# The memory update of a segmented attention block: one full-array product for a group of heads, or one column tile for each head's quadrant

## The chip, the cores and the metric

The kernel runs on one core of a Trainium2 chip. The core has TensorE (PE, with its weight loads as a row of their own, PEld), VectorE (DVE), ScalarE (ACT), GpSimd (POOL) and SyncE (SP, which only issues DMAs). The metric is the device time of one execution in microseconds, as a median over runs. Profiles come from one execution each.

## The reference

A pre-norm transformer block on 2048 tokens of 640 values: attention with 32 heads of 20 values, in four segments of 512 tokens, and a feed-forward part of 1728. Inside a segment the attention is a causal softmax; what earlier segments had is read through a memory M (20 x 20 a head) and its normaliser z, which are updated after each segment.

```python
phi = lambda t: jnp.where(t > 0, t + 1.0, jnp.exp(t))
for s in range(N):
    logits = jnp.einsum('bhqd,bhkd->bhqk', qs, ks) * scale + mask
    a_dot = jnp.einsum('bhqk,bhkd->bhqd', _softmax(logits, axis=-1), vs)
    pq = phi(qs)
    num = jnp.einsum('bhld,bhde->bhle', pq, M)
    den = jnp.einsum('bhld,bhd->bhl', pq, z)[..., None] + 1e-06
    outs.append(g * num / den + (1.0 - g) * a_dot)
    pk = phi(ks)
    M = M + jnp.einsum('bhld,bhle->bhde', pk, vs)
    z = z + jnp.einsum('bhld->bhd', pk)
h = x + concat(outs) @ wo
h2 = h + silu(layernorm(h) @ w1) @ w2
```

## The kernel before

**Layout.** The projections q and k put the 640 values into five tiles of 128 rows. A tile has four quadrants of 32 rows; quadrant r of tile c holds the 20 values of head 4c+r and 12 rows out of the heads 20 to 31, which are cut into pieces. `Vx` holds the values of a segment with a column of ones behind each head (VS = 21 columns a head, V4 = 84 for four heads), so that one product gives M and z.

**The work of a segment.** Layer norm and transposes (n1_), projections of v (v), q and k (pr), their evacuation (qe), phi of q and k (ex on ACT, then pa and pb on DVE, L844 and L850), eight ticks of four heads, the output projection (wo, rs), a second layer norm (n2_), and the feed-forward part (h1, th, s, h2, o, out). A tick has scores (qk, L900), their exponentials (e, ACT, L913), the causal masks (mk, POOL, L925), the product with the values (av, L948), its scaling (oe, L963), the transposition together with the reading of the memory (tn, L977 and L981) and the normalisation (nm, ad).

**The memory update**, `declare_memory`, once after each of the segments 0, 1 and 2, for each of the five tiles c: a DMA transpose of phi(K) into `phiKt` (kt, L1049, on SP's queue), four products (mz, L1057; eight for c = 4), one addition into the running sum `Mz` (ma, DVE; L1083 copies in segment 0, L1086 adds later), and one product with a constant mask `MzM` on POOL that writes the bf16 operand `Mzb` of the next segment's ticks (mb, L1093). A product takes a whole tile, 128 columns of phi(K) transposed, as weights and moves the values of two or three groups of four heads (168 or 252 columns) through it. So each quadrant meets the values of all four heads of a group, and the mask then keeps only the blocks where a quadrant met its own head. Each tile has a PSUM bank of its own for this and an `Mz` buffer of its own.

**The order.** There is no scheduler at run time. Each piece of work is a task with a name, such as `mz03` (segment 0, tile 3) or `ma03`; the string `ORDER` lists all of them, with the buffer slots and, after a slash, the engine (`/A` ACT, `/D` DVE, `/G` POOL, `/S` SP). Each engine gets its instructions in the order of the list and waits in order; semaphores come from a tracker of reads and writes. `/C` marks a TensorE task that is written as column tiles: each full-array matmul (128*128, L545) becomes four on 32 columns each (128*32, L546) that lie side by side in the array. The scores use row tiles (20*128), av and the last h1 of a segment column tiles, the rest the full array.

Of the kernel before, what the change touches and what calls it, by code (L numbers as in the profile page):

```python
# [327 lines left out]
D = 640  # L328
# [34 lines left out]
zpad:0 iota epsc vpad1 mt0 x0:0 mta0 mtb0 halfc sel mt3 n1_st0:6 x1:1 n1_rs0 n1_st1:1 x2:2 x3:3 w_q:0 n1_st2:3 n1_rs1  # L363
n1_rs2 n1_st3:5 fill20:0 n1_rs3 re_wq0/G:0 re_wq1/G n1_ap1:0 n1_ap2:2 mm2 w_k mt1 warm:0 re_wk1/G:0 fill9:0 n1_tp1:4
mm9 re_wk2/G n1_ap0:3 n1_ap3:0 w_wv:0 n1_tp2:2 n1_tp0:0 mm6 n1_tp3:6 n1_te3/D:2 vpad0 mta3 beta n1_te1/A n1_te2/A mta1
re_wq2/G n1_te0/A re_wk0/A x4/A:4,5,6,7 mtb3 re_wk3/G pr000.0:6 pr000.1 qe000/A:0 pr010.0:1 pr001.0:2 re_wk4/A pr001.1
qe001/D pr011.0:7 pr011.1 zf0 zf1 mm8 qe011/D:0 pa011:1 re_wq3/G qk0a0:4,2 lsc0 lsc1 x8/A:8,9,10,11 ex001:1 re_wq4/G
pa001:2 pb001 kt00:0 mzc9 e0a0:4 pr010.1 qe010/D e0a2 mtb1 pr021.0:7 pr021.1 qe021/D:0 n1_st4:4 n1_rs4 v00.0:6 pa021:0
ex011:2 qk0b0:3,1 e0b0:5 e0b2 mk0b w_w1_3/S:0 w_w1_4/S pb011 v01.0:0 mm1 n1_st5:5 v00.1 ve00/A:0 pr020.0:5 pr020.1
qe020/A v01.1 n1_rs5 vt09:0 ex021:1 vt03 w_w2_5/S qk0e0:2,6 e0e2:0 v02.0:4 v02.1 v03.0:6 e0e0 n1_st6:6 ve01/D ve02/A  # L370
n1_st9:1 qk1a0:2,0 n1_ap5:2 n1_rs6 v03.1 n1_ap6:0 e1a0:1 pr031.0:4 pr031.1 kt01:1 n1_tr5:0 vt00 e1a2 n1_tr6 ve03/D
qk1b0:2,5 e1b0:6 e1b2 pb021 qe031/D:0 w_w1_0/S pr030.0:7 pr030.1 n1_ap4:3 n1_tr4 pr041.0:4 mk1a qk2a0:2,0 n1_st10:3
lsc2 mzc6 pa031:1 qe030/D pr041.1 qe041/D:0 ex031:1 pr040.0:5 pr040.1 vt06 e2a2:3 qe040/D vt08 vt04 e2a0 qk2b0:6,0
e2b0:2 vt07 lsc3 mk0e mk1b mz00:4 mk0a ma00/D:0 pb031 vt02 n1_rs10 av1:3 e2b2 oe1/D:1 mm5 mm11 mzc5 av0:2 oe0/D:0 mm0
qk2e0:4,6 e2e0:6 mz01:0 ma01/D:2 tn0:2 qk3a0:4,0 e2e2 mt2 e3a2:0 nm0:1,0 tn1:3 nm1:1 v10.0:2 v10.1 mk2b n1_st7:5
ve10/D:1 kt02:0 e3a0 mk2a n1_st11:6 qk3b0:0,6 mk2e vt05 e3b2:1 n1_rs7 e3b0 vt01 av2:5 oe2/D:1 mm3 mk3a qk4a0:6,2
mz02:4 ma02/D:3 mk3b v11.0:0 e4a2:2 vt010 e4a0 qk4b0:2,4 n1_rs9 mta2 mm4 n1_ap7:3 n1_st8:5 n1_rs8 kt03:1 e4b0:4 e4b2
vt011 v11.1 ve11/D mk4b tn2:7 nm2:1 pa041:2 mz03:6 ex041:2 qk4e0:2,0 e4e0:3 av3:7 e4e2 mk4a n1_tr7 epsg0 pr100.0/C:4
pr100.1/C ma03/D:4 oe3/D:0 qk5a0:2,6 mzc1 e5a0:5 mk4e pr110.0:5 pb041 e5a2 kt04:0 qe100/D:0 pr110.1 pr120.0:4
qe110/D:0 qk5b0:2,0 pa110:0 mtb2 av4:5 oe4/D:1 pa100:0 pr120.1/C mzc2 n1_ap10:3 n1_tr10:2 e5b2:6 qk6a0:0,6 w_w1_1/S  # L380
mz04:5 qe120/D:0 e5b0 ma04/D:1 v12.0:2 tn3:4 nm3:2 n1_ap8:1 e6a2:4 v12.1 ve12/D e6a0 tn4:7 ex100:1 pb100 nm4:2
qk6b0:4,0 pr101.0:6 e6b2:0 mk5b pr101.1 e6b0 qk6e0:0,2 e6e2:1 mk5a av5:7 n1_rs11 pa120:0 mzc0 e6e0 pr111.0/C:4 qe101/D
w_w2_3/S pr111.1/C qk7a0:2,5 e7a0:3 e7a2 n1_ap9:3 oe5/D:0 pr130.0:7 n1_tr8 qe111/D tn5:0 pa111:2 mm7 v13.0:4 nm5:2
pr130.1 qe130/D:0 qk7b0:2,0 mzc7 mzc3 mb01:0 mk6b v13.1/C ex111:1 pb111 mk6e mk6a av6:6 n1_tr9 mzc4 ve13/D e7b2:5
pr140.0/C:7 pr140.1/C qk8a0:0,4 pa101:1 oe6/D:0 pr121.0:6 pr121.1 e7b0 qe140/D:0 tn6:7 ex101:2 ex120:0 pb101 mb02:0
pb120 e8a0:4 mk7b e8a2 qk8b0:2,0 w_wo/S:0 e8b2:0 e8b0 mk7a qe121/D av7:6 nm6:0 pr131.0/C:7 oe7/D:1 kt10:1 qk8e0:0,4
e8e2:6 tn7:6 pa130:0 kt11:0 nm7:0 pr131.1/C qe131/D e8e0 mz11:2 ma11 qk9a0:5,3 mzc8 pr141.0:7 w_w2_4/S n1_ap11:3
vt10:0 mb03:0 e9a2:3 e9a0 ot0:1 mk8b mz10:1 ot1 mb00:0 ma10 pr141.1 pa121:0 mk8e qk9b0:0,2 e9b2:1 wo0.0:4 wo0.1 mk8a
av8:2 e9b0 mk9b ex131:2 qe141/D qk10a0:0,6 mk9a rs0 oe8/D:0 wo1.0:3 wo1.1 e10a0:2 e10a2 n2_st0:5 rs1 n2_st1:2 ot2
wo2.0:2 n2_rs0 ex110:0 qk10b0:0,5 e10b2:5 vt110 wo2.1 rs2 ot3 wo3.0:4 e10b0 wo3.1 pa131:2 ex121:1 qk10e0:2,0 e10e2:0  # L390
v20.0:6 v20.1 n2_rs1 n2_ap1:2 v21.0:0 e10e0 w_w1_2/S pb131 pb121 rs3 ve20/A:0 vt13 qk11a0:4,2 vt17 vt19 e11a0:4
n2_st2:1 vt15 v21.1 v22.0:6 tn8:4 e11a2 n1_tr11 n2_tr1:1 pb110 mk10a ex141:0 mk10b v22.1 w_w2_0/S n2_st3:7 n2_ap0:0
epsg1 nm8:3,1 vt16 v23.0:2 vt12 n2_rs2 ve22/A v23.1 n2_ap2:1 mk10e ve21/A ex140:2 n2_rs3 qk11b0:6,4 av9:0 ve23/D
ex130:1 e11b2:6 n2_ap3:3 oe9/D:1 av10:1 mzc11 vt14 oe10/D:0 pb130 e11b0 pr201.0/C:2 pr201.1/C qk12a0:0,4 e12a2:2
qe201/D:0 ex201:1 mk11a e12a0 mm10 tn9:6 n2_tr0 pr211.0:3 pr211.1 n2_tr2 n2_tr3 tn10:4 mzc10 mb04:0 ad8:0 nm9:3,0
qe211/A:0 nm10:0,1 vt11 pa141:1 h1_0_0_0.0:2 h1_0_0_0.1 mk11b av11:6 pa140:0 th0_0_0:0 s0_0_0:0 oe11/D:0 pb141
qk12b0:0,3 h1_0_1_0.0:7 h1_0_1_0.1 ad9 kt12:1 mz12:5 kt13:0 mz13:6 vt18 e12b2:1 tn11:2 e12b0 th0_1_0:1 vt111 ma12 ma13
qk12e0:4,0 e12e0:4 pr221.0:6 e12e2 ad10 s0_1_0 pr221.1 h1_0_2_0.0:7 h1_0_2_0.1 nm11:0,1 th0_2_0:0 qk13a0:3,1 e13a2:0
h1_0_3_0.0:5 mk12a mk12b h1_0_3_0.1 qe221/D:0 e13a0 pa211:2 pa201:0 pb201 mk12e kt14:0 mz14:6 pr231.0:2 s0_2_0 av12:7
ma14 th0_3_0:1 mk13a ex211:0 oe12/D:0 qk13b0:3,0 e13b0:2 e13b2 mk13b pr231.1 h1_0_4_0.0:6 s0_3_0 h1_0_4_0.1 th0_4_0:0  # L400
qe231/D:0 qk14a0:2,4 e14a2:1 w_w2_1/S h1_0_5_0.0:7 pb140 tn12:0 h1_0_5_0.1 e14a0 s0_4_0 pr200.0:6 pr200.1 th0_5_0:0
nm12:3,0 qk14b0:0,3 qe200/D s0_5_0 e14b0:3 av13:2 oe13/D:0 h1_0_6_0.0/C:5 h1_0_6_0.1/C qk14e0:1,6 e14b2 pr241.0:0
pr241.1 qe241/D:0 ad12 th0_6_0:1 h1_0_7_0.0:4 h1_0_7_0.1 e14e2:5 tn13:6 e14e0 s0_6_0 qk15a0:0,2 mk14b th0_7_0:0
e15a0:2 h1_0_8_0.0:5 e15a2 h1_0_8_0.1 s0_7_0 th0_8_0:0 nm13:2,0 mk14a h1_0_9_0.0:4 pb211 h1_0_9_0.1 pr210.0:7
qk15b0:0,2 mk14e av14:6 s0_8_0 pr210.1 oe14/D:1 ex200:1 e15b0:4 th0_9_0:1 s0_9_0 h1_0_10_0.0:1 kt20:0 h1_0_10_0.1
e15b2 ad13 mk15a qe210/D h1_0_11_0.0:0 qk16a0:4,2 th0_10_0:0 s0_10_0 tn14:6 nm14:1,0 h1_0_11_0.1 e16a2:0 e16a0
th0_11_0:0 h1_0_12_0.0:1 h1_0_12_0.1 th0_12_0:1 pa200:0 pb200 mk15b ad11 s0_11_0 qk16b0:6,3 e16b2:3 av15:5 oe15/D:1
pr220.0/C:2 pr220.1/C s0_12_0 e16b0 qe220/D h1_0_13_0:3 th0_13_0:0 pa221:0 s0_13_0 kt21:1 pa231:2 qk16e0:6,0 e16e0:5
tn15:4 pr230.0:2 ad14 nm15:2,0 pa210:0 pr240.0:3 e16e2 pr230.1 qk17a0:6,0 qe230/D mz20:4 mk16a mb10:0 ex221:0 ma20
e17a0:1 pr240.1/C mk16b qe240/D e17a2 mb11:0 mk16e qk17b0:4,6 e17b2:6 av16:2 ad15 mz21:3 pa240:0 oe16/D:0 mk17a  # L410
# [54 lines left out]
def build(nc, es, A_x, A_wq, A_wk, A_wv, A_wo, A_beta, B_x, B_w1, B_w2, out):  # L465
# [70 lines left out]
    def dve_c(n):  # L536
        return n / 960.0 + 0.067
# [172 lines left out]
    def layer_norm(tag, b, xa, xsub, dstA, i, prio):  # L710
# [31 lines left out]
        if tag == "n1_" and b < 4:  # L742
# [528 lines left out]
```

## Time and profile before

| | before |
|---|---|
| median of 3 runs | 301.94 us (301.9 to 303.04) |
| the profiled execution | 301.67 us |
| its span | 299.9 us |
| granted TensorE clock over the span | 1.00 |
| memory products, L1057 | 72 of 128x84 to 128x252, mean 200 to 270 ns each |
| additions, L1083 and L1086 | 15, of 168 or 252 elements, 5.4 us busy |
| masks, L1093 | 15, of 168 or 252 elements (542 and 719 ns), 9.2 us busy |
| transposes of phi(K), L1049 | 15, landing 3.2 us after their issue (median; 2.3 to 6.8) |

The length of a matmul row holds the time until its last result has landed, so matmuls overlap in the rows; what one costs the stream is the distance between the starts. Times in a timeline are counted from the start of the span. A row that begins with a line number gives the line, the engine, the operation, what it writes and reads, its tile shape (rows*columns of the array) and its data shape.

### The profile page before, as it was taken

Reading aid. Unit: us, or ns where it says so; the run is one execution under the profiler, and the core shown is the slowest. Engines: PE = TensorE matmul, PEld = TensorE weight load, DVE = VectorE, ACT = ScalarE, POOL = GpSimd, SP = SyncE. Lnnn points to the kernel's source line nnn. Section 1 sums busy time; section 2 is a strip of 40 time slices with the busy share of each in tenths; the row PEclk is TensorE's granted clock in tenths of the full one; section 3 lists DMA queues with packets and bytes.
Section 4 is the critical chain, followed back from the end, with each engine's and each line's share of the span. In section 5 each row is a group of like instructions: output and inputs, shape, how many; then the busy total and the mean of one; then the engine's idle time right before and its main releaser. Section 6 shows DMA issues by size and latency. Waiting matters only on the chain.

```text
span 299.9 us, 7708 instructions
## 1 busy us (share of the span) xinstructions
PE 284.8 (95%) x3134; PEld 158.7 (53%) x3160; DVE 222.5 (74%) x460; ACT 212.6 (71%) x273; POOL 150.0 (50%) x299
## 2 busy tenths in 40 slices
PE   8799889989989999999999999999999999999996
PEld 5354444435545444566654454555654557764574
DVE  6498988987999868879968975698545777726622
ACT  3699999999988999975788768877888741004400
POOL 5896886674665355746563752445863621300000
PEclk9999999999999999999999999999999999999999
DMA  7787524936663103064447220601511013321021
GB/s 212 260 258 115 118 48 103 216 75 150 166 101 89 20 2 87 5 96 80 80 93 125 46 44 7 112 2 23 61 40 30 2 48 65 71 63 44 1 90 44
DMA packets 48579, 24.68 MB, mean 82 GB/s; under 512 B 38880, under 2 KB 47456, under 8 KB 48544
## 3 DMA queue, kind: packets, MB, share of 16 engines
q1 hardware_dynamic: 47488, 22.88, 35.2%
q10 hardware_dynamic: 1056, 1.31, 1.4%
q8 instruction: 25, 0.41, 0.6%
q14 instruction: 10, 0.08, 0.1%
HBM read 10.41 MB, written 2.62 MB: 43 GB/s over the span
## 4 chain that ended last, share of the span: by engine, by line
PE 70%; DVE 14%; DMA 6%; ACT 6%; issue 2%; SPq 1%; POOL 0%; DVEq 0%; ACTq 0%
PE ps_all L545 48%; PE ps_all L546 6%; PE ps_all L900 6%; PE ps_all L948 4%; ACT PT L913 4%; DMA sT<-in_A_wk_dram 3%; DVE stt L720 2%; DMA x_tok<-in_A_x_dram 2%; PE ps_all L977 2%; DVE x_tok L1125 1%; PE ps_all L1057 1%; PE ps_all L981 1%; DVE sT L1166 1%; DVE phiQ L850 1%; DVE xn_rot L737 1%
## 5 line engine op out<-in xcount | busy, mean ns | idle before, releaser
L913 ACT ACTIVATE PT<-ps_all 128x1024 bf16<-128x1024 f32 x160 | 154.9, 1028 | 27.6 <-PE ps_all L900 24.7
L925 POOL TENSOR_SCALAR_AFFINE_SELECT PT<-PT 128x512 bf16<-128x512 bf16 x128 | 82.1, 648 | 63.2 <-ACT PT L913 59.9
L1160 ACT ACTIVATE th<-ps_all 128x512 f32<-128x512 f32 (+1 forms) x56 | 32.1, 591 | 35.9 <-PE ps_all L545 28.8
L545 PE MATMUL ps_all<-tT,w_sb 128*128 128x512 bf16 x224 | 53.8, 380 | 1.5 <-issue 0.5
L545 PE MATMUL ps_all<-w_sb,sT 128*128 128x320 bf16 x376 | 53.9, 299 | 0.0
L1166 DVE SCALAR_TENSOR_TENSOR sT<-th,ps_all 128x512 bf16<-128x512 f32 (+1 forms) x56 | 36.2, 662 | 16.9 <-ACT th L1160 16.3
L545 PEld LDWEIGHTS ps_all<-w_sb,sT 128*128 128x128 bf16 x376 | 35.9, 98 | 15.6 <-issue 1.5
L545 PEld LDWEIGHTS ps_all<-tT,w_sb 128*128 128x128 bf16 x233 | 21.0, 98 | 26.1 <-issue 2.8
L720 DVE BATCH_NORM_STATS2 stt<-x_tok 128x6 f32<-128x320 bf16 x64 | 28.0, 479 | 2.2 <-DMA x_tok<-in_A_x_dram 1.8
L1202 DVE SCALAR_TENSOR_TENSOR x_tok<-ps_all,x_tok 128x640 bf16<-128x640 f32 (+1 forms) x17 | 13.2, 781 | 19.9 <-PE ps_all L545 14.7
L1022 POOL TENSOR_TENSOR otok<-on 128x320 bf16<-128x320 bf16 x24 | 19.2, 801 | 12.7 <-DVE on L1014 12.7
L545 PE MATMUL ps_all<-wv_sb,tT 128*128 128x320 bf16 x155 | 24.3, 300 | 0.2
L963 DVE TENSOR_SCALAR oTs<-ps_all,lsc 128x512 bf16<-128x512 f32 x29 | 21.4, 744 | 3.8 <-PE ps_all L948 3.5
L545 PE MATMUL ps_all<-wo_sb,tT 128*128 128x320 bf16 x160 | 23.6, 299 | 0.6 <-DMA tT<-otok 0.6
L948 PE MATMUL ps_all<-PT,Vx 128*32 128x384 bf16 (+3 forms) x512 | 22.7, 301 | 1.2 <-DVE QK L831 0.7
L831 DVE CAST QK<-ps_all 128x512 bf16<-128x512 f32 x26 | 17.8, 686 | 7.0 <-PE ps_all L545 6.9
L1014 DVE TENSOR_TENSOR on<-ps_all,rd 128x640 bf16<-128x640 f32 x24 | 19.8, 825 | 1.3 <-POOL otok L1022 0.5
L729 POOL TENSOR_TENSOR rst<-mvt,eps_c 128x1 f32<-128x1 f32 x32 | 6.6, 207 | 27.8 <-DVE mvt L723 27.7
L545 PE MATMUL ps_all<-tT,wqr 128*128 128x512 bf16 x70 | 18.1, 379 | 2.2 <-DVE tT L756 1.2
L545 PE MATMUL ps_all<-tT,wkr 128*128 128x512 bf16 x72 | 18.8, 379 | 1.3 <-issue 1.1
L731 POOL TENSOR_TENSOR rst<-rst,eps_c 128x1 f32<-128x1 f32 x32 | 18.0, 563 | 2.5
L545 PEld LDWEIGHTS ps_all<-wo_sb,tT 128*128 128x128 bf16 x160 | 15.0, 98 | 7.8 <-issue 1.1
(86 smaller groups left out, 356.4 us busy)
## 6 DMA issues: line engine op xcount, KB each, us to landing
out_dram<-x_tok SPq DMA_DIRECT2D x15, 160.0 KB, 1.9
w_sb<-in_B_w_dram SPq DMA_DIRECT2D x5, 432.0 KB, 4.0
w_sb<-in_B_w_dram SPq DMA_DIRECT2D x3, 480.0 KB, 3.9
x_tok<-in_A_x_dram ACTq DMA_DIRECT2D x2, 640.0 KB, 4.9
QKV<-QK SPq DMA_DIRECT2D x12, 72.0 KB
sT<-in_A_wq_dram SPq DMA_DIRECT2D x1, 800.0 KB, 6.2
sT<-in_A_wk_dram SPq DMA_DIRECT2D x1, 800.0 KB, 8.0
wv_sb<-in_A_wv_dram SPq DMA_DIRECT2D x1, 800.0 KB, 9.6
```

The costliest lines, as they stand in the source:

```text
L545: return [lambda e: e.matmul(out, lhsT=lhsT, rhs=rhs, start=start, stop=stop)]
L546: return [lambda e, p=p: e.matmul(out[p:p + 32, :], lhsT=lhsT[:, p:p + 32], rhs=rhs, start=start, stop=stop, tile_position=(0, p)) for p i ...
L720: T.add(DV, lambda e, hh=hh: e.bn_stats(out=stt[:, s, 6 * hh:6 * hh + 6], in_=xb[:, 320 * hh:320 * hh + 320]), reads=R((xa, xsub)), writes ...
L731: T.add(PO, lambda e: e.tensor_tensor(out=rst[:, s, :], in0=rst[:, s, :], in1=eps_c[:, 1:2], op=ALU.pow), reads=R((st, ["r"]), (C, ["half" ...
L913: T.add(AC, lambda e: e.activation(out=pt[:, pta.slot, q0:q0 + 2, 0:width], in_=sc3[:, b0:b0 + 2, 0:width], func=ACT.Exp, scale=SCALE), re ...
L925: fns.append(lambda e, v=v: e.affine_select(out=v, in_=v, pattern=[[0, 4], [1, 128]], compare_op=ALU.is_ge, fill=0.0, base=0, channel_mult ...
L948: fns.append(lambda e, j=j, r=r, h=h, pa=pa, pt=pt, co=co, q0=q0, ji=ji: e.matmul(bank(po)[32 * r:32 * r + 32, q0:hi], lhsT=Vx[:, vx.slot, ...
L963: f = lambda e: e.tensor_scalar(out=o, in0=i_, scalar1=lsc[:, g:g + 1], scalar2=None, op0=ALU.mult)
L1014: T.add(DV, lambda e: e.tensor_tensor(out=on[:, ona.slot, :, :].rearrange("p b (x e) -> p b x e", e=DH), in0=v[:, :, :, 0:DH], in1=r2.unsq ...
L1022: T.add(PO, lambda e: e.tensor_tensor(out=o_dst, in0=on[:, ona.slot, 0, :].rearrange("p (i x) -> p i x", i=4), in1=on[:, ona.slot, 1, :].r ...
L1160: T.add(AC, lambda e: e.activation(out=th[:, tha.slot, lo:hi], in_=bank(ps)[:, lo:hi], func=ACT.Tanh, scale=0.5), reads=R((ps, [0])), writ ...
L1166: T.add(DV, lambda e: e.scalar_tensor_tensor(out=sT[:, f, lo:hi], in0=th[:, tha.slot, lo:hi], scalar=1.0, in1=bank(ps)[:, lo:hi], op0=ALU. ...
```

## The change

In `declare_memory` the four products of a tile become products in column tiles. A quadrant r of the transposed phi(K), 32 columns of `phiKt`, is the weight of one column tile, and only the values of its own heads move through it: two, three or one heads, 42, 63 or 21 columns. The four quadrants are written one after the other in the program as a group of four. Their results go to the rows 32r to 32r+31 of one PSUM bank, side by side with those of the other tiles: 12 pieces of 21 columns for the whole segment. One addition of 252 elements takes the bank into one `Mz` buffer, which is now [128, 12, 21] in place of [128, 12, 84] and is one allocation for all five tiles. The mask products on POOL have the same number and the same output; each reads its piece of `Mz` four times over, by a broadcast, against the same mask.

One detail is not a matter of shape: for the tiles 0 to 2 the product before moved the groups that begin with the heads 4c and 4c+20, and the new one moves the heads 4c+r and 4c+16+r. So the memory rows of these pieces of the heads 20 to 31 are computed with other heads' values. The count and the size of the instructions are the same for either.

The pools change from two to five buffers for `phiKt` and from five to one for `Mz`. The list `ORDER` is another one from its first to its last line. In it 106 projections and feed-forward parts carry `/C`, against 38; two of the loads of x stand on SP's queue in place of ACT's; six copies that rearrange the weights of q and k go to DVE.

```diff
-        "pK": 3, "ex": 3, "pKt": 2, "Vx": 2, "Mz": 5, ...
+        "pK": 3, "ex": 3, "pKt": 5, "Vx": 2, "Mz": 1, ...
-    Mz = sb("Mz", [128, 12, V4], F32)
+    Mz = sb("Mz", [128, 12, VS], F32)
...
+        ps = G.alloc("ps", 1)
         for c in range(5):
             pkt = G.alloc("pKt")
...
-            def e_mm(eng, c=c, pkt=pkt, ps=ps, nb=nb):
...
-                for i in range(4):
-                    v = Vx[:, vx.slot, i, 0:H * VS]
-                    if c < 3:
-                        rhs = v[:, V4 * c:V4 * c + 6 * V4].rearrange("p (a x) -> p a x", x=V4)[:, 0:6:5, :]
-                        fns.append(mm(i, rhs, 0, 2 * V4, i == 0, i == 3))
...
-            G.task(f"mz{s}{c}", {PE: 4 * pe_c(V4 * nb)}, e_mm, [(pkt, [0]), (vx, list(range(4)))], [(ps, [0])],
-                   pr + P["mz"], mode="f")
+            def e_mm(eng, c=c, pkt=pkt):
+
+                heads = [(4 * c, 16, 2)] if c < 3 else [(12, 8, 3)] if c == 3 else [(16, 8, 2), (28, 1, 1)]
+                fns, o0 = [], VS * MZB[c]
+                for h0, st, nh in heads:
                     for i in range(4):
+                        v = Vx[:, vx.slot, i, 0:H * VS].rearrange("p (h e) -> p h e", e=VS)
+                        for r in range(4):
+                            fns.append(lambda e, i=i, r=r, v=v, h0=h0, st=st, nh=nh, o0=o0: e.matmul(
+                                bank(ps)[32 * r:32 * r + 32, o0:o0 + VS * nh],
+                                lhsT=phiKt[:, pkt.slot, i, 32 * r:32 * r + 32],
+                                rhs=v[:, h0 + r:h0 + r + st * (nh - 1) + 1:st, :],
+                                start=(i == 0), stop=(i == 3), tile_position=(0, 32 * r)))
+                    o0 += VS * nh
...
+            G.task(f"mz{s}{c}", {PE: 0.22}, e_mm, [(pkt, [0]), (vx, list(range(4)))], [(ps, [c])],
+                   pr + P["mz"], mode="c")
+        acc = Mz[:, :, :]
+
+        def e_acc(eng):
+            pv = bank(ps)[:, 0:12 * VS].rearrange("p (a x) -> p a x", x=VS)
...
+                T.add(DV, lambda e: e.tensor_tensor(out=acc, in0=pv, in1=acc, op=ALU.add),
+                      reads=R((ps, [0]), (MZ, [0])), writes=R((MZ, [0])))
...
+        G.task(f"ma{s}", engs, e_acc, [(ps, list(range(5)))] + ([(MZ, [0])] if s else []), [(MZ, [0])], pr + 0.7)
+        for c in range(5):
+            nb, mb = MZN[c], MZB_A[s + 1][c]
+
+            def e_mb(eng, c=c, nb=nb, mb=mb):
+                b0 = MZB[c]
+                T.add(PO, lambda e: e.tensor_tensor(
+                    out=Mzb[:, b0:b0 + nb, :].rearrange("p a (r x) -> p a r x", r=4),
+                    in0=Mz[:, b0:b0 + nb, :].unsqueeze(2).to_broadcast([128, nb, 4, VS]),
+                    in1=MzM[:, b0:b0 + nb, :].rearrange("p a (r x) -> p a r x", r=4), op=ALU.mult),
+                      reads=R((MZ, [0]), (C, [f"mm{q}" for q in range(b0, b0 + nb)])), writes=R((mb, [0])))
```

Three places of the list where the update of the memory stands now:

```text
qe110/D:0 pr100.1/C mz00:4 mz01 e5a2 mm4 kt03:3 pr120.0/C:1 mk4b
av4:5 qe120/D:0 pa120:0 n1_rs9 oe4/D:0 n1_ap9:1 n1_tr11:1 mz02 mz04 e5b0 w_w1_2/S:0 mz03 ma0/D:0
s0_4_0 mz13 mk12b mk12a av12:5 h1_0_5_0.1/C mb04:0 ma1 pr231.0/C:7 oe12/D:0
```

## The prediction

> **What bounds the kernel now.** I read the page's engine shares first, then the chain of work that ended last, then busy time by stretch, then TensorE's rows in order of time around the memory products, and last the rows of the tile Mz.
>
> ```profile
> PE 284.8 (95%) x3134; PEld 158.7 (53%) x3160; DVE 222.5 (74%) x460; ACT 212.6 (71%) x273; POOL 150.0 (50%) x299
> ...
> PE 70%; DVE 14%; DMA 6%; ACT 6%; issue 2%; SPq 1%; POOL 0%; DVEq 0%; ACTq 0%
> ```
>
> TensorE is busy for 95% of the span and is 70% of the chain, so time taken out of its stream is worth something; but 30% of the chain is elsewhere. Where that is, the stretches tell (columns: length, then busy time of PE, weight loads, DVE, ACT and POOL):
>
> ```profile
> 20.00:60.00 40.00, 36.93 (x469) 18.40 (x473) 35.47 (x83) 39.22 (x47) 29.64 (x67) 1.00 0.60 133
> 60.00:90.00 30.00, 26.54 (x317) 14.46 (x320) 26.59 (x57) 27.03 (x34) 18.72 (x36) 1.00 0.60 123
> 90.00:225.00 135.00, 132.59 (x1642) 72.97 (x1647) 105.44 (x216) 110.44 (x138) 73.12 (x122) 1.00 0.30 56
> ```
>
> From 20 to 60 us, in segment 0, ACT is busy for 39.22 of 40 us and TensorE for 36.93: there the exponentials bound the time, and a shorter TensorE task only makes a longer pause. From 60 to 90 us three engines stand near 90% and wait for each other. From 90 us on TensorE alone is full (132.59 of 135). What the memory products cost is read off TensorE's rows, by the distance from one row's start to the next (a row's own length has the pipeline's tail in it):
>
> ```profile
> 121.75 1.46 PE L545 MATMUL ps_all<-tT,wqr 128*128 128x512 bf16 x6
> 123.14 0.40 PE L900 MATMUL ps_all<-QK 20*128 20x512 bf16 x4
> 123.47 0.46 PE L1057 MATMUL ps_all<-Vx,phiKt 128*128 128x168 bf16 x4
> 123.86 0.83 PE L546 MATMUL ps_all<-tT,wqr 128*32 128x512 bf16 x12
> 124.75 0.40 PE L900 MATMUL ps_all<-QK 20*128 20x384 bf16 x8
> 125.08 0.73 PE L948 MATMUL ps_all<-PT,Vx 128*32 128x512 bf16 x16
> 125.74 0.46 PE L1057 MATMUL ps_all<-Vx,phiKt 128*128 128x168 bf16 x4
> 126.05 1.25 PE L545 MATMUL ps_all<-w_sb,sT 128*128 128x320 bf16 x8
> 127.13 0.31 PE L977 MATMUL ps_all<-Mzb,phiQ 128*128 128x84 bf16 x4
> 127.28 0.32 PE L981 MATMUL ps_all<-ident,oTs 128*128 128x84 bf16 x4
> 127.53 0.40 PE L900 MATMUL ps_all<-QK 20*128 20x512 bf16 x4
> 127.86 1.81 PE L546 MATMUL ps_all<-w_sb,sT 128*32 128x320 bf16 x48
> 129.50 0.71 PE L948 MATMUL ps_all<-PT,Vx 128*32 128x512 bf16 x16
> 130.15 0.40 PE L900 MATMUL ps_all<-QK 20*128 20x384 bf16 x8
> ```
>
> Four products of 168 columns take 0.31 us (125.74 to 126.05). The same four take 0.39 us at 123.47, because the next row is in another tile shape (128*128, then 128*32): a change of shape costs about 0.1 us. Column tiles run four side by side: 12 groups of four with 320 columns take 1.64 us (127.86 to 129.50), 0.137 a group, against 1.08/8 = 0.135 for one full product of 320 columns.
>
> **The change, part by part.** *TensorE's products.* Before, a segment has three tiles of four 168-column products (0.31 us each), one of four 252-column products and one of eight; the last two take 0.43 us (rows at 169.74 and 170.17) and 0.44 us (96.87 and 97.31). That is 3 x 0.31 + 0.43 + 0.44 = 1.80 us a segment, 5.4 us in three. After, each of the 72 products becomes a group of four column tiles with 21, 42 or 63 columns. No row shows so narrow a group. Low end: column tiles cost time by their columns alone; a segment's 24 groups have 16 x 42 + 4 x 63 + 4 x 21 = 1008 columns, at 0.137 us/320 = 0.43 ns a column 0.43 us, so 1.3 us in all. High end: the narrowest group in the trace has 128 columns, and at the same rate takes 0.055 us, so 72 x 0.055 = 4.0 us. I take the row with the nearest width, the 84-column step (127.13 to 127.28, 0.15/4 = 0.0375 us): 72 x 0.0375 = 2.7 us. Off TensorE: 2.7 us (1.4 to 4.1).
>
> *What of it is hidden.* A third, segment 0's 0.9 us, stands in the new list where the old one has it, among the second half of segment 0's ticks, in the stretch that ACT bounds; I count it as nothing. It counts if the order finds other TensorE work to put there. That leaves -1.8 us.
>
> *Changes of tile shape.* Counted along the two lists (qk in row tiles; av, entries with /C, the last h1 of a segment and now mz in column tiles; the rest on the full array) there are 180 before and 182 after: mz now stands in runs, or next to /C work. +0.2 us. The Trainium skill, page "TensorEngine Tiling (Array Packing)", section Tiling Modes, says that changing the tiling mode drains the array. The 0.1 us above agrees; were each of the 15 tasks alone among full-array work, two changes each, it would be 30 x 0.1 = 3.0 us, more than the gain, and the list's neighbours are what keeps that out.
>
> *Entries that turn into column tiles.* 106 projections and feed-forward parts instead of 38: 720 more matmuls, so 240 groups; at 0.137 against 0.135 each that is 0 to 0.5 us; +0.2 us.
>
> *DVE.* These rows go down to three instructions of 252 elements:
>
> ```profile
> L1086 DVE TENSOR_TENSOR Mz<-ps_all,Mz x10: 317/332/420, 65.6 to 170.8; 128x168 f32<-128x168 f32 x6, 128x252 f32<-128x252 f32 x4
> L1083 DVE COPY Mz<-ps_all x5: 322/333/414, 30.6 to 48.7; 128x168 f32<-128x168 f32 x3, 128x252 f32<-128x252 f32 x2
> ...
>   PEld ps_all L900: 1.3, 3
>   PEld ps_all L545: 0.8, 2
> ```
>
> 15 instructions took 5.4 us (by stretch 1.81, 0.66, 2.13 and 0.82 us); three at 0.41 take 1.2. DVE is not full, so the 4.2 us count only where somebody waited: TensorE's loads did, 1.3 + 0.8 = 2.1 us in five places. Some 0.5 of that is five changes of shape, which stay; of the other 1.6, 12 of 15 evacuations go: 1.3 us at most, nothing at least. I take half, -0.6 us, as a part lies before 60 us.
>
> *POOL and the single Mz.* The 15 mask products (542 and 719 ns) stay, now reading a broadcast tile. Bounds: 0 to a doubling, 9.2 us on POOL, which is 50% busy; they lie under other POOL pauses (59.9 us of waiting for ACT), so I count 0; without that cover the tick's product in L977 comes up to 0.7 us late each. But Mz is one buffer now: the addition ma1 may not write before mb04, the last mask of segment 0, has read. In the list mb04 stands straight ahead of ma1, behind the masks mk12b and mk12a on POOL. Queued behind ma1 on DVE are oe12 and nm12, for which tick 12's TensorE work waits. POOL's waits for ACT are 41 with 59.9 us, 1.5 us in the mean, 3.8 the longest; I take 0 and keep 3.8 for the range.
>
> *DMA.* The same 15 transposes, five buffers for two. Two loads of x go from ACT's queue to SP's, ahead of every transpose; ACT loses two issues of 0.4 us. DVE takes six weight copies of some 0.5 us from ACT and POOL, in the first 15 us, where it waits 3.2 us for TensorE at w_sb L831. Nothing for either; if that cover is gone, the first scores come 0.5 us late.
>
> **The sum.** -1.8 + 0.2 + 0.2 - 0.6 = -2.0 us. The profiled run took 301.67 us (span 299.9 and 1.8 around it), so 299.7; the runs' median is 301.94, 0.3 above it, so 299.9 us as a median. No difference means within 0.5%, about 1.5 us: 300.4 to 303.4.
>
> **The rivals.** (a) *Nothing is hidden and narrow groups go by columns*: -4.1 + 0.2 - 1.3 gives 296.7 us. For it: TensorE is 70% of the chain. Against it: the 20 to 60 us row. (b) *The pause moves*: the saved time becomes waiting for ACT and DVE in the reordered middle, as between 60 and 90 us where no engine is full; 301.2 to 301.9 us, no change. For it: TensorE stands idle for 3.1 and 3.5 us in the two early stretches already, and every entry of the list has a new neighbour, so that a pause can as well be born. (c) *Slower: DVE stands at ma1 until POOL has masked mb04.* With the longest wait of POOL's row, 3.8 us, the stall reaches DVE, then the bank of tick 12, then the exponentials: 299.9 + 3.8 = 303.7 us. It decides from 3.5 us on; below that it ends in (b). For it: a wait that wasn't there, between two queues in order. Against it: the two masks ahead are 0.65 us each and POOL idles half the time. (d) *The column tiles don't run side by side when narrow*: 288 matmuls at the 84-column step, 10.8 us for 5.4, +5.4 - 0.6 + 0.4 gives 307.1 us. Against it: the row of 16 at 129.50 has 128-column members and lasts 0.65 us with its change of shape, so that its 1280 columns go at the plain rate. The Trainium skill, page "TensorE: Matmul & The Clock Gate", Part 1, states that start to start never falls below about 25 ns; taken a matmul that would be 288 x 25 ns = 7.2 us, an estimate, and the kernel 1.8 us longer. That row gives 35 ns a matmul, so no row settles it.
>
> **Chances.** Forecast 0.44 (0.38 below 300.4, 0.06 above), (a) 0.12, (b) 0.23, (c) 0.16, (d) 0.05. Faster 0.38 + 0.12 = 0.50; same 0.06 + 0.23 = 0.29; slower 0.21. Range 297.0 to 303.8: it leaves out half of (a), (d) and what (c) brings beyond its one wait.
>
> **What would show it.** Groups of L1057's successor 0.02 to 0.055 us apart; three Mz rows of 0.41 us; DVE's pause before the second of them under 1 us; about 1.8 us less between 90 us and the end. I am wrong if that stretch keeps its length although the products shrank, if a pause over 2 us stands before Mz on DVE, or if groups are over 0.1 us apart.

## The result and the profile after

| | before | after |
|---|---|---|
| median of 10 runs, taken side by side | 303.2 us (301.26 to 304.43) | 300.7 us (299.9 to 301.68) |
| ratio, with its 95% interval | | 0.9925 [0.9903, 0.9946] |
| the profiled execution, and its span | 301.67 us, 299.9 us | 301.27 us, 299.5 us |
| memory products | 72 on the full array | 288 column tiles, 72 groups of four |
| evacuations into `Mz` | 15, 5.4 us | 3, 1.24 us |
| all instructions | 7708 | 9583 |

The changed kernel is 0.75% faster, 2.5 us in the medians. The two profiled executions differ by only 0.4 us: before's is among the fastest of its runs, after's is the second slowest of ten. So the pair of profiles shows what the steps cost, but the gain as a whole has to be read from many runs.

The page after, its engine shares:

```profile
PE 281.5 (94%) x4069; PEld 158.7 (53%) x4096; DVE 223.3 (75%) x455; ACT 211.5 (71%) x271; POOL 146.5 (49%) x294
```

TensorE has 935 more matmuls and is busy for 3.3 us less. The three stretches, with the columns as before:

```profile
20.00:60.00 40.00, 35.62 (x639) 17.75 (x643) 36.56 (x82) 37.85 (x44) 27.94 (x58) 1.00 0.72 140
60.00:90.00 30.00, 26.82 (x425) 15.00 (x428) 27.31 (x58) 26.90 (x34) 18.15 (x39) 1.00 0.56 113
90.00:225.00 135.00, 131.58 (x2266) 73.35 (x2270) 104.21 (x209) 111.58 (x140) 74.82 (x127) 1.00 0.34 58
```

From 20 to 60 us TensorE is busy for 1.3 us less and ACT for 1.4 us less than before: there the order differs, and ACT has its own pauses. From 90 us on TensorE is nearly as full as it was. TensorE's rows in order of time at the products of segment 2:

```profile
169.01 0.80 PE L1063 MATMUL ps_all<-Vx,phiKt 128*32 128x42 bf16 x80
169.72 0.86 PE L547 MATMUL ps_all<-wv_sb,tT 128*32 128x320 bf16 x20
```

Eighty matmuls are 20 groups, 21 to 63 columns wide and 42 in the mean (the row names its first form only). From their start to the next row's, in the same tile shape, it is 0.71 us: 0.0355 a group. The 16 groups of segment 0 (47.36 to 48.00 us, with one change of shape of 0.1) took 0.034 each. A segment's 24 groups cost 0.8 us, against 1.80 for the 24 products before. The tile Mz (operation and count, then min/median/max in ns, first and last start):

```profile
L1081 DVE TENSOR_TENSOR Mz<-ps_all,Mz x2: 408/414/421, 99.0 to 170.5; 128x252 f32<-128x252 f32 x2
L1078 DVE COPY Mz<-ps_all x1: 413/413/413, 48.6 to 48.6; 128x252 f32<-128x252 f32 x1
...
  PEld ps_all L547: 0.2, 1
```

Three rows of 0.41 us, as forecast, and TensorE's loads wait for them for 0.2 us where it was 2.3 (1.3 and 0.8, and 0.2 at L948). Was DVE held up at the single `Mz`? POOL's row, and then DVE's rows around ma1:

```profile
98.13 0.68 POOL L1090 TENSOR_TENSOR Mzb<-Mz,MzM 128x252 bf16<-128x252 f32 x1
```

```profile
97.53 1.29 DVE L1166 SCALAR_TENSOR_TENSOR sT<-th,ps_all 128x512 bf16<-128x512 f32 x2 [1.75 <-ACT th L1160]
98.96 0.42 DVE L1081 TENSOR_TENSOR Mz<-ps_all,Mz 128x252 f32<-128x252 f32 x1
```

The mask mb04 ends at 98.81 us, DVE's work ahead of ma1 at 98.82, and ma1 starts at 98.96. The pause is 0.14 us.

The profiled execution after was 1.1 us ahead of before's at 86 us and at 128 us (starts of the same exponential, counted along ACT), and 1.4 us behind it at 138 us. In between, TensorE waited for a transposed tile of the attention's output.

```profile
136.66 1.54 PE L547 MATMUL ps_all<-wo_sb,tT 128*32 128x320 bf16 x40 [0.77 <-DMA tT<-otok]
```

ACT stood for 3.42 us before its row at 135.94. From 143 us to the end the two stay within about 1 us of each other. This wait is not peculiar to one execution: of the kernels below, "heads20", "seg2 wide" and "start filled" have 0.56 to 0.70 us in front of the same row; "seg0 wide" and "new list, wide products" have none. The list of transfers in the traces tells the two kinds apart. In the four traces with the wait, a 16 KB packet of the queue that brings instructions (q8 on the page) started while the transpose was under way, and the transpose took 4.4 to 4.5 us. In the two without it, no packet came, or only 0.14 us before the landing, and the transpose took 2.72 us.

### The profile page after: what moved, and what is told of

Its sections match the earlier page's. It is cut to its first block, busy times and chain, and to the rows that moved or that the text cites. A ratio compares the mean times of both kernels' runs of the same rounds, so it can differ in the third digit from the quotient of the medians.

```text
span 299.5 us, 9583 instructions
## 1 busy us (share of the span) xinstructions
PE 281.5 (94%) x4069; PEld 158.7 (53%) x4096; DVE 223.3 (75%) x455; ACT 211.5 (71%) x271; POOL 146.5 (49%) x294
## 4 chain that ended last, share of the span: by engine, by line
PE 72%; DVE 11%; ACT 9%; DMA 4%; issue 2%; SPq 1%; POOL 0%; ACTq 0%; DVEq 0%; POOLq 0%
PE ps_all L546 38%; PE ps_all L547 17%; ACT PT L914 8%; PE ps_all L901 6%; PE ps_all L949 4%; PE ps_all L616 2%; PE ps_all L978 2%; DMA tT<-otok 1%; DMA tT<-xn_rot 1%; DMA phiKt<-phiK 1%; PE ps_all L982 1%; DVE on L1015 1%; DVE QK L832 1%; DVE phiQ L851 1%; DVE xn_rot L738 1%
## 5 line engine op out<-in xcount | busy, mean ns | idle before, releaser
L546 PE MATMUL ps_all<-w_sb,sT 128*128 128x320 bf16 x360 | 52.1, 300 | 0.0
L546 PEld LDWEIGHTS ps_all<-w_sb,sT 128*128 128x128 bf16 x360 | 34.3, 98 | 14.8 <-issue 1.5
L546 PE MATMUL ps_all<-tT,w_sb 128*128 128x512 bf16 x161 | 37.5, 379 | 1.0 <-DVE sT L1166 0.3
L546 PEld LDWEIGHTS ps_all<-tT,w_sb 128*128 128x128 bf16 x172 | 15.9, 98 | 18.2 <-DVE sT L1166 1.1
L547 PE MATMUL ps_all<-tT,w_sb 128*32 128x512 bf16 x352 | 22.4, 380 | 0.0
L832 DVE CAST QK<-ps_all 128x512 bf16<-128x512 f32 x25 | 17.0, 683 | 4.1 <-PE ps_all L546 2.6
L738 DVE TENSOR_SCALAR xn_rot<-x_tok,mvt,rst 128x640 bf16<-128x640 bf16 x32 | 16.6, 534 | 2.9 <-POOL rst L732 1.9
L546 PE MATMUL ps_all<-wv_sb,tT 128*128 128x320 bf16 x120 | 18.3, 300 | 0.3 <-ACT PT L914 0.2
L949 PEld LDWEIGHTS ps_all<-PT,Vx 128*32 128x32 bf16 x512 | 12.0, 96 | 10.8 <-issue 2.6
L901 PE MATMUL ps_all<-QK 20*128 20x512 bf16 (+3 forms) x240 | 15.1, 301 | 2.6 <-DVE QK L832 1.2
```

What stands on the lines that cost most here:

```text
L546: return [lambda e: e.matmul(out, lhsT=lhsT, rhs=rhs, start=start, stop=stop)]
L547: return [lambda e, p=p: e.matmul(out[p:p + 32, :], lhsT=lhsT[:, p:p + 32], rhs=rhs, start=start, stop=stop, tile_position=(0, p)) for p i ...
L832: (lambda e: e.tensor_copy(out=o, in_=i_))
L901: fns.append(lambda e, j=j, o=o, r=r, q0=q0, q1=q1, qa=qa, ka=ka: e.matmul(ps_all[:, o:o + q1 - q0], lhsT=ka[32 * r:32 * r + DH, 128 * j:1 ...
L949: fns.append(lambda e, j=j, r=r, h=h, pa=pa, pt=pt, co=co, q0=q0, ji=ji: e.matmul(bank(po)[32 * r:32 * r + 32, q0:hi], lhsT=Vx[:, vx.slot, ...
```

## The experiments

Medians are compared with runs of the kernel before on the same chip. The kernels were measured in five batches, not all on one chip, and the medians of before in them go from 302.51 to 303.46 us, so kernels of different batches are better compared by their ratios. In the expectations, e1 is "heads20", e6 is "code, old list", and the theories A to D are stated where they first come.

Some run-to-run steps can be read from the mean granted clock of a run: half clock for 3.41 us lowers a mean over 300 us by 0.0057, and runs come with 1.000, 0.994, 0.989 or 0.984, or 0.001 less. "Clock lost" below counts the runs under 0.995. For the kernel before, the runs with one such stretch have a median 0.5 to 2.2 us above the runs with none (303.6 and 303.1 us, 304.4 and 302.3, 303.9 and 302.4, 304.8 and 302.7 in four batches). The kernel before lost it in 19 of 82 runs.

| kernel | list | products | start filled | median us | ratio to before | clock lost |
|---|---|---|---|---|---|---|
| after | new | column tiles | no | 300.7 | 0.9925 [0.9903, 0.9946] | 0 of 10 |
| heads20 | new | column tiles | no | 300.89 | 0.9895 [0.9863, 0.9928] | 1 of 6 |
| start filled | new | column tiles | yes | 300.18 | 0.9919 [0.9897, 0.9942] | 0 of 6 |
| new list, wide products | new | full array | yes | 301.84 | 0.9979 [0.9958, 0.9999] | 0 of 12 |
| before, start filled | old | full array | yes | 301.79 | 0.9967 [0.9947, 0.9987] | 1 of 12 |
| products alone | old | column tiles | no | 304.73 | 1.0059 [1.0019, 1.01] | 6 of 12 |
| code, old list | old | column tiles | no | 305.89 | 1.0073 [1.004, 1.0107] | 9 of 12 |
| the same, filled at 67 us | old | column tiles | no | 303.63 | 1.0045 [1.002, 1.0069] | 3 of 12 |

"Products alone" and "code, old list" share a batch, so do "new list, wide products" and "before, start filled", and so do "start filled", "the same, filled at 67 us" and the two kernels with few large matmuls below.

**The second heads.** The stride of the second group goes back to what the kernel before computes.

```diff
-                heads = [(4 * c, 16, 2)] if c < 3 else ...
+                heads = [(4 * c, 20, 2)] if c < 3 else ...
```

> The changed kernel with the stride of the second head at 20, as the products before had it; nothing else differs. Both theories expect the changed kernel's time: ratio to the kernel before 0.9925 within 0.003. It is the base for the three runs beside it.

Measured: 300.89 us, 0.9895 [0.9863, 0.9928], which overlaps after's. No cost of the detail can be told, and all kernels of the new code below have the stride 20.

**Products four times over.** The products of one segment are issued four times into the same bank.

```diff
-                T.run(PE, fns, ...)
+                T.run(PE, fns * (4 if s == 0 else 1), ...)
```

> Segment 0's column-tile products (tiles mz00 to mz04) are issued four times over, each time from zero, so the result is the same; 3 x 0.8 us = 2.4 us more TensorE time between 45 and 48 us, where ACT was the full engine. Theory A (product time in that stretch lies under ACT's exponentials): at most 0.6 us above the base. Theory B (every TensorE microsecond counts, wherever it stands): 2.4 us above the base.

> The same with segment 2's products, which stand near 167 and 170 us, where TensorE alone is full: 2.4 us more TensorE time there. Theories A and B both expect 2.0 to 2.4 us above the base. A third one, C (the saved product time became waiting anyway, and the gain comes from the new list): under 1 us above the base.

Measured: 309.59 us (1.0178 [1.0142, 1.0214]) and 311.07 us (1.0254 [1.0228, 1.028]). Neither theory gave such prices; the experiment measured something else. TensorE's rows of the second kernel in order of time (in brackets: the idle time before a row, and what ended it):

```profile
170.50 1.21 PE L1063 MATMUL ps_all<-Vx,phiKt 128*32 128x42 bf16 x128 [0.81 <-issue]
173.96 1.19 PE L1063 MATMUL ps_all<-Vx,phiKt 128*32 128x42 bf16 x127 [2.25 <-issue]
177.52 1.53 PE L547 MATMUL ps_all<-wv_sb,tT 128*32 128x320 bf16 x20 [2.37 <-issue]
```

TensorE takes 128 matmuls in 1.2 us and then stands for over 2 us with nothing to wait for that the profile shows. From start to start it is 3.46 and 3.56 us. 128 matmuls with their 128 weight loads are 256 instructions. The pages count the packets of the instruction queue, 16 KB each: 25 before, 32 after and 35 in this kernel. That is 10 packets for the 2446 TensorE instructions that this kernel has more than before, some 250 a packet, so the stops come once a packet. The list of transfers in the traces has the packets in time: each of the six stops marked "issue" at the memory products of the two kernels, of 0.81 to 3.06 us, ends 1.2 to 1.5 us after such a packet has come in. So TensorE outran the supply of its own instructions; no run changed that supply by itself. The clock was half for 6.83 us from 175.13 us on. Many tiny matmuls in a row are therefore no measure of where time is hidden, and the next pair uses few large ones.

**Work added at the products, few instructions.** 4 groups of 512 and 8 of 256 columns, 1.73 us of TensorE, beside the products of segment 0 ("seg0 wide") or of segment 2 ("seg2 wide").

```diff
+                if s == 0 and c in (0, 2):
+                    for q0, n in [(0, 512)] * 4 if c == 0 else [(256, 256)] * 8:
+                        for r in range(4):
+                            fns.append(lambda e, ...: e.matmul(bank(ps)[32 * r:32 * r + 32, q0:q0 + n],
```

> e1 with 1.73 us more TensorE time at segment 0's products and few instructions: four groups of column tiles with 512 columns and eight with 256, into columns of the bank that are not used or are written again later. The two x4 runs had added hundreds of instructions and TensorE stood waiting for its own instructions there, so they did not measure this. Theory A (this stretch is bound by ACT): at most 0.5 us above e1. Theory B (every TensorE microsecond counts): 1.7 us.

> The same 1.73 us at segment 2's products, in the stretch where TensorE is full. Theories A and B: 1.5 to 1.7 us above e1. Theory C (saved time there became waiting): under 0.7 us.

Measured: 300.64 us, 0.9941 [0.9906, 0.9977], with the work in segment 0; 302.3 us, 0.9976 [0.9946, 1.0005], in segment 2. The exponentials tell it more sharply. Against after's trace, the added work in segment 2 moves them by 1.45 us at its place (from 0.32 to 1.77), and they stay there to the end: 84% is kept. In segment 0 it moves them from -0.73 us just ahead of the work (at 45 us) to +0.65 behind it (at 49 us), 1.38 of 1.73, and 1.21 of that is left at 127 us. ACT's rows there, with the added work and then in after:

```profile
47.03 1.94 ACT L914 ACTIVATE PT<-ps_all 128x1024 bf16<-128x1024 f32 x2 [0.79 <-PE ps_all L901]
49.40 2.97 ACT L914 ACTIVATE PT<-ps_all 128x1024 bf16<-128x1024 f32 x3 [0.43 <-PE ps_all L901]
```

```profile
46.92 5.84 ACT L914 ACTIVATE PT<-ps_all 128x1024 bf16<-128x1024 f32 x6
```

ACT waits for TensorE's scores for 1.22 us where it had no wait. So some 0.5 us of the 1.73 lies under the exponentials, and the rest does not: theory A's price fails at the place itself. The medians, 1.7 us apart, are no sign of hiding either. "Seg0 wide" is the kernel without the wait at 136 us, and in its trace the exponentials gain 1.26 us on after's there.

**The column-tile entries.** All `/C` marks are taken off the list.

```diff
-wo0.0/C:4 wo0.1/C e9b0 pa140:0 ex120:1
+wo0.0:4 wo0.1 e9b0 pa140:0 ex120:1
```

> The same list with every /C taken off, so that 106 projections and feed-forward parts run on the full array again; the changes of tile shape along the list go from 182 to 212. If a change of shape costs the stream 0.1 us and four column tiles cost what one full product costs: 30 x 0.1 = 3.0 us above the base, less what of it lies in waits (2 to 3 us). If column tiles cost time of their own (more instructions): 1 to 2 us at most, or below the base.

Measured: 301.52 us, 0.9932 [0.9906, 0.9957], against 0.9895 [0.9863, 0.9928] of heads20: 0.6 us in the medians, and the intervals overlap. In the trace the 30 more changes of shape are there, at 0.1 us each in the median (the distance of the starts, less what the last product takes among its own kind), but TensorE's other pauses shrink by some 2.6 us. The marks are worth at most a fraction of what their changes of shape cost; what they cost instead was not taken apart.

**Products alone.** The old kernel with its list, banks and fifteen additions; only the products are column tiles and the additions narrower.

```diff
-                        fns.append(mm(i, rhs, 0, 2 * V4, i == 0, i == 3))
...
+                        for r in range(4):
+                            fns.append(lambda e, ...: e.matmul(bank(ps)[32 * r:32 * r + 32, o0:o0 + VS * nh], ...,
+                                start=(i == 0), stop=(i == 3), tile_position=(0, 32 * r)))
```

> The kernel before with its own list, banks and 15 additions; only the products are column tiles, and the additions have 42 or 63 elements. TensorE's products fall from 5.4 to 2.4 us (-3.0), the changes of tile shape rise from 180 to 191 (+1.1), the additions shrink by some 0.1 us each. Theory A, a third of both hidden in segment 0: -1.0 to -1.5 us, ratio 0.995 to 0.997. Theory C (the new list makes the gain): 0.

Measured: 304.73 us, 1.0059 [1.0019, 1.01]. Slower, which neither theory had. TensorE's rows of this kernel:

```profile
44.54 0.30 PE L900 MATMUL ps_all<-w_sb 20*128 20x256 bf16 x4 [2.13 <-DMA QKV<-w_sb]
...
46.02 2.29 PE L546 MATMUL ps_all<-tT,wqr 128*32 128x512 bf16 x20
```

and the same 20 projections in the kernel before:

```profile
42.58 1.25 PE L546 MATMUL ps_all<-tT,wqr 128*32 128x512 bf16 x20
```

A product is followed by a wait of 2.13 us for a transfer, and behind it the same 20 projections take 2.29 us for 1.25: the granted clock is half from 44.70 to 48.11 us. It was half from 10.57 to 13.98 us as well. Six of the twelve runs have such a stretch. That is not all of it: the six without one take 302.5 to 304.87 us, where before takes 301.48 to 303.5, and for this no reason was found.

Why that transfer came so late can be read from the traces. The transfers under way from 41.8 to 43.4 us in this kernel (for a queue: packets, MB, share of 16 engines; for an issue: how many, and the us to landing):

```profile
q8 instruction: 1, 0.02, 6.2%
...
tT<-xn_rot SPq DMA_TRANSPOSE x1, 4.4
```

and the same transpose in the kernel before, with no row of q8 in its window from 40.2 to 41.8 us:

```profile
tT<-xn_rot SPq DMA_TRANSPOSE x1, 2.6
```

The instruction packet takes 1.60 us from 41.92 us on, and packets of 256 bytes, 0.02 us at 40 us, take up to 1.89 us beside it. The awaited transfer had been issued at 39.98 us; its last two pieces landed at 44.27 and 44.30 us, all others by 42.06. That the packet held them up is read from these times and was not tried by itself.

**After's code under the old list.** The products of a segment stand together where the last one stood, with one addition.

```diff
-mz00:4 mk0a ma00/D:0 pb031 ...
+mk0a pb031 ...
...
-ot0:1 mk8b mz10:1 ot1 mb00:0 ma10 pr141.1 ... qk9b0:0,2 e9b2:1 wo0.0:4
+ot0:1 mk8b ot1 mb00:0 pr141.1 ... qk9b0:0,2 e9b2:1 wo0.0:4
```

> The changed code (one bank, one addition a segment, one Mz) in the old list: a segment's five products stand together where its last one stood, the addition where the last addition stood, and everything else is where it was; 182 changes of shape. Theory A: -2.0 us, the changed kernel's ratio of 0.9925 within 0.003. Theory C: 0 or slower, since the gain is the new list's.

Measured: 305.89 us, 1.0073 [1.004, 1.0107]. TensorE's rows where segment 1's first products used to stand:

```profile
70.03 1.95 PE L536 MATMUL ps_all<-wo_sb,tT 128*128 128x320 bf16 x10 [2.06 <-DMA tT<-otok]
```

and in the kernel before:

```profile
68.30 1.53 PE L545 MATMUL ps_all<-wo_sb,tT 128*128 128x320 bf16 x10 [0.64 <-DMA tT<-otok]
```

The transfer ends the wait in both. It was issued 0.36 us later than before's (65.75 against 65.39 us), but landed 1.73 us later (69.98 against 68.25): an instruction packet started at 67.23 us, while it was under way; none did in before. So most of the longer wait, 2.06 us for 0.64, is the transfer's own delay. The clock is half from 70.99 to 74.41 us.

**That wait filled.** 14 products on zeros ahead of wo0.0, whose results nobody reads.

```diff
-qk9b0:0,2 e9b2:1 wo0.0:4
+qk9b0:0,2 e9b2:1 fill14:4 wo0.0:4
```

> e6 (the changed code in the old list) with 14 products of zeros, 1.5 us of TensorE work that computes nothing, ahead of the first output projection, where e6 stood idle for 2.06 us and then ran 3.4 us at half its clock. Theory D (in the old list the shorter products leave a pause long enough to drop TensorE's clock, and that costs more than they save): 1.0 to 2.0 us FASTER than e6, although work is added. Without D: as e6, or up to 1.5 us slower.

Measured: 303.63 us, 1.0045 [1.002, 1.0069]: 2.3 us less than without the added work in the medians, but from another batch; by the ratios it is 0.3%, and the intervals overlap.

```profile
67.03 1.70 PE L606 MATMUL ps_all<-zpad 128*128 128x256 bf16 x14
69.16 1.53 PE L536 MATMUL ps_all<-wo_sb,tT 128*128 128x320 bf16 x10 [0.43 <-DMA tT<-otok]
```

The pause is 0.43 us and the ten products take 1.53 us again. Runs with lost clock go from 9 in 12 to 3 in 12. So a pause of some 2 us costs its own length and then, through the clock, about 1.5 us more (the unfilled kernel's eight runs with one stretch have a median of 306.06 us, its three with none 304.58). The clock isn't all: the filled kernel's runs at full clock have 303.5, and for this other 1.1 us the traces give no reason.

**The start filled, in the new list.** heads20's trace has such a pause, which ends at 11.49 us (2.16 us, for the rearranged weights), so 8 products on zeros go ahead of the first projections.

```diff
-n1_te3/A n1_te2/D pr020.0/C:0 w_wv:0
+n1_te3/A n1_te2/D fill8:2 pr020.0/C:0 w_wv:0
```

> e1 with 8 such products, 0.85 us, in the pause before the first projection. In e1's profile the weights came late, that pause was 2.16 us long, and the clock stood at half from 12.46 to 15.88 us; in the changed kernel's own profile it was 0.88 us and the clock stayed full. Theory D, for the start: the runs' spread shrinks (e1 299.0 to 302.5) and the median falls by 0.3 to 1.0 us. Without it: no change, or 0.3 us slower.

Measured: 300.18 us, 0.9919 [0.9897, 0.9942], runs from 299.42 to 300.94 where heads20's went from 299.04 to 302.51. The median is not told apart from after's.

**The fourth corner: the new list with full-array products.** The filled kernel, one bank and three additions, but 72 full products; they are written over one another, so the memory holds other values.

```diff
-                        for r in range(4):
-                            fns.append(lambda e, ...: e.matmul(bank(ps)[32 * r:32 * r + 32, o0:o0 + VS * nh], ...
+                        fns.append(lambda e, ...: e.matmul(bank(ps)[:, 0:V4 * ng], lhsT=phiKt[:, pkt.slot, i, :],
+                            rhs=v[:, g0:g0 + st * (ng - 1) + 1:st, :], start=(i == 0), stop=(i == 3)))
```

> The new list, the one bank and the single additions, with the filler at the start as in the run before, but the 72 products are full-array matmuls of 84 to 252 columns again, written over one another in the one bank (the memory then holds other values; only the time is looked at). This is the fourth corner beside 'products alone' and 'code under the old list'. TensorE's stream grows by the products' 3.0 us and by four changes of shape of 0.095 us, 3.4 us in all. If the products' saving is what the new list keeps (segment 0's third absorbed, segments 1 and 2 kept at four fifths, as the added work showed): 1.8 to 2.8 us above the same kernel with column-tile products, so 302.0 to 303.0 us, level with before. If the list alone made the gain and products are worth nothing: within 0.6 us of 300.2 us, a ratio of about 0.993 to before.

Measured: 301.84 us, 0.9979 [0.9958, 0.9999], 1.66 us above the same kernel with column tiles (300.18, 0.9919 in another batch; the intervals lie apart, and by the ratios it is 1.8 us). That is about the lower end of the range expected for "the products' saving is kept" and outside that of "the list alone". Segment 2's products here, and the row behind them:

```profile
168.90 1.61 PE L1062 MATMUL ps_all<-Vx,phiKt 128*128 128x168 bf16 x20
170.44 0.86 PE L547 MATMUL ps_all<-wv_sb,tT 128*32 128x320 bf16 x20
```

1.54 us for 20 products and a change of shape, against 0.70 for the 20 groups in the filled kernel. Between these two traces the exponentials move apart at the products of every segment: by 0.95 us in segment 0 (from -1.35 at 47 us to -0.40 at 50), by 0.97 around segment 1's and by 0.51 around segment 2's. The two are nearly level from the start (-0.14) to 56 us (-0.41) only because the filled kernel had lost 1.2 us just ahead of segment 0's products, with a TensorE pause of 1.64 us from 41.90 us on, for a tile of DVE (oTs), which the other has not. Ten exponentials, from the start of the 25th to that of the 35th, take 10.06 or 10.07 us in the five traces of this list with marks, column tiles and nothing added in segment 0 (after, heads20, start filled and two with work added in segment 2), and 10.90 with full products.

**The start filled, in the old list.**

```diff
-re_wk3/G pr000.0:6 pr000.1
+re_wk3/G fill8:6 pr000.0:6 pr000.1
```

> The kernel before, with eight matmuls on zeros ahead of its first projections and nothing else. About three in ten runs of the kernel before show a mean granted clock of 0.994 or 0.989 (one or two stretches of 3.4 us at half clock) and take 1.5 us more for each. If the start, where TensorE waits for x and its norm, is where the clock is lost: no run under 0.999, and a median of 302.2 to 302.6 us, ratio 0.996 to 0.999. If it is lost elsewhere (around 45 or 70 us, where TensorE waits for transfers): still a quarter of the runs under 0.995, and a median within 0.4 us of the kernel before.

Measured: 301.79 us, 0.9967 [0.9947, 0.9987], lower than either side expected. One run lost clock in spite of the filling. In this batch only 2 of 23 runs of before had, too few to explain 0.9 us, and the filled kernel's other runs (median 301.62) are lower than before's (302.65) as well. So the start of the old list costs something that eight idle products take away, and what it is stays open.

## Why the prediction was right, and where not

*The whole.* 299.9 us was forecast (297.0 to 303.8) and 300.7 measured, a gain of 2.0 us forecast and 2.5 measured. The sign and the size hold. That the size came out so near is in part luck, as the terms show.

*Products, -2.7 us, of which segment 0's 0.9 hidden.* The price is right: a group, 42 columns in the mean, takes 0.034 to 0.0355 us, where the 84-column row gave 0.0375; 72 groups cost 2.5 us instead of 5.4. In one and the same list the column tiles are worth 1.66 us in the medians (1.8 by the ratios), against the -1.8 counted. The hidden third is not borne out in the new list: around segment 0's products the exponentials of the fixed-list pair move apart by 0.95 us, as much as around segment 1's, and of the work added there 1.2 us of 1.73 came through. The three places of that pair add up to 2.4 us; why the medians keep only 1.7 was not shown. So the -1.8 agrees, but the step that led to it, "I count it as nothing", does not.

The profiled pair spreads the gain over other lengths: from the 61st exponential to the end it takes 213.5 us before and 214.2 after, so the sign "1.8 us less between 90 us and the end" failed as it was put. With the list held fixed that stretch is 214.7 us with full products and 213.3 with column tiles, 1.4 us; but after and heads20, with the same products, have 214.2 and 214.1, so one pair of traces does not settle its size.

*Shape changes, +0.2.* Right: there are 180 and 182 in the traces, at 0.105 us each in the median.

*Entries that became column tiles, +0.2.* The groups do take 0.137 us for 0.136. But the term left out that the marks keep 30 changes away. Taking all 106 off, and not only the new ones, moves the median by only 0.6 us; the sign of their net worth was not settled.

*DVE, -0.6 us.* Not confirmed. TensorE's waits for `Mz` went from 2.3 to 0.2 us, yet list, bank and three additions together give nothing once both starts are filled (301.84 against 301.79 us). The runs do not separate the additions from the list.

*POOL, counted as nothing.* Right: the 15 masks take 543 ns in the median where they took 544.

*What the sum lacked.* Some 0.8 us of the 2.5 came from elsewhere. Against the kernel before without filling, the new list with full products and a filled start is 0.8 us faster (302.67 to 301.84), and the filling alone does the same for the old list; in the new list it changes nothing that can be told. So this part is one that idle work ahead of the first projections also brings, and not the memory update's; what it consists of stays open. The prediction had no term for it, and -0.6 us for DVE, which is not confirmed, stands at about its size. Its base, 301.94 us from three runs, lay 1.3 us under the median of the ten now shown. It had no term for the transfer of instructions either: after has 32 packets of them for 25, and a transpose that meets one lands 1.2 us later in the median.

*The rivals.* (c) fell: DVE paused for 0.14 us at ma1. (d) fell: four matmuls of 42 columns in the mean took 0.035 us, 9 ns each. The Trainium skill, page "TensorE: Matmul & The Clock Gate", Part 1, has 25 ns as the least from start to start; taken per matmul that does not hold for column tiles in the bursts of this case, taken per column tile it does, within 1 ns (24 ns at the least). (a) fell by its price, since a group takes 0.034 us or more where columns alone would give 0.018; its other half, that nothing is hidden, is nearer to the traces of the new list than the forecast's third. (b) was not what happened in the new list, but in the old one the saving was lost, and worse than (b) was priced: products alone are 0.6% slower there. In the traces of the old list, transfers that met an instruction packet came late; at 44 and 70 us the waits for them passed 2 us and brought half clock. Why the old list is slower in its runs at full clock too stays open. The prediction saw neither the packets nor that a longer wait can cost clock.

## What to carry to other kernels

In a list with a fixed order, the worth of a shorter task depends on what stands around it: try the edit with the list fixed and the list with the edit undone, since here the same products gave -1.7 us in one list and +1.4 in the other. Count the instructions that an edit adds, and see which transfers their packets meet. Look at each TensorE pause that grows towards 2 us, and put work there, even idle work. Price narrow column tiles by groups of four from the nearest narrow row, and issue them in short bursts. When two traces are compared at one place, take the distance just ahead of it and just behind it: from a point further off, another pause can cancel what is looked for.

## What the runs showed of the hardware

**Half clock after short pauses.** The traces' record of the clock begins at 3.8 to 8.5 us. From there on, in the traces of all kernels, TensorE stands for over 2 us in six places (2.06, 2.13, 2.16, 2.25, 2.37 and 3.06 us). At each of them the clock is half within 1.2 us of the pause's end, for 3.41 us or, at the two stops close together, 6.83. At the pauses of 1.51, 1.64, 1.73 and 1.88 us it stays full. All stretches of half clock begin a whole number of steps of 3.413 us after the first row of the clock in their trace (1, 2, 11, 14, 19 and 49 steps), so the idle time within a step is the better measure. TensorE was idle for 2.06 to 2.86 us in six of the seven steps that half clock follows, and for 1.73 us at most in all the others; the pause of 1.88 us lay across two steps, with 1.47 and 1.46 us idle in them. The seventh is the step ahead of 10.57 us in "products alone", with 1.53 us and no pause over 1.0 us. The Trainium skill, page "TensorE: Matmul & The Clock Gate", Part 1, has a free-running window of 3413 ns and lets the clock fall after an idle one; the stretches' length and their grid agree, but pauses well under a window were enough here.

**A supply limit for instructions.** 128 matmuls with 128 weight loads passed in 1.2 us, but over several such bursts only in 3.5 us: 27 ns a matmul sustained against 9 ns in a burst. The Trainium skill, page "Runtime: NRT & Kernel Launch", section "Instruction fetch mechanics", describes refills of 256 instructions and calls them mostly hidden; the count agrees with the spacing of the stops, the hiding did not hold for this burst.

**Transposes that meet an instruction packet.** In the fourteen traces together, 194 DMA transposes had a 16 KB instruction packet start within 2.2 us of their issue; they took 3.87 us to land in the median, the other 630 took 2.64.

**A least distance for each column tile.** In the eleven traces with memory products in narrow column tiles, two products on the same column tile start 24 ns or more apart. At the head of a burst it is 25 ns, with 21 columns as with 42; after some 28 matmuls in a row it is about 33 ns, 8 ns a matmul, whatever the width.
